# Two 64x64 steps in one slot, and a w_out product that lags two FFN steps

## The chip, the cores and the metric

The kernel runs on one core of a Trainium2 chip. The metric is the device time of one execution in microseconds (us); the time before is the median of three runs. A core has a matrix engine (TensorE, in the profile PE, with its weight loads as PEld), three engines for everything else (VectorE or DVE, ScalarE or ACT, GpSimd or POOL), and SyncE (SP), which here only issues transfers. Each engine works through its own list of instructions in order and waits on semaphores for the others. TensorE writes to PSUM; VectorE and ScalarE read the results from there.

## The reference

A long convolution of each channel, made from a small filter network, is followed by a feed-forward block (FFN) with three input products and a maximum. Four sequences of 12544 positions, 128 channels, all in fp32:

```python
h_filt = (np.maximum(pos_emb @ w1, 0.0) @ w2) * window      # one filter per channel
u = x * v
y = irfft(rfft(u, n=2*S, axis=1) * rfft(h_filt, n=2*S, axis=0), n=2*S, axis=1)[:, :S, :]
a = (x * y).reshape(B * S, D)                               # 50176 x 128
h = np.maximum(np.maximum(a @ moe_w1, a @ moe_w2), a @ moe_w3)   # 50176 x 768
out = h @ moe_w_out                                         # 50176 x 128
```

The kernel computes the transforms as matrix products, in several steps of which one, in the frequency domain, is done in blocks of 64x64. The maximum of three is turned into a maximum of two: one input product is subtracted from the weights of the other two ahead of time, and its own share of the output is one further product with a matrix `lin`.

## The kernel before

The program has a prologue (filter, transforms of sequence 0), a middle stage, and a last stage (the FFN of sequence 3). In the middle stage the FFN of sequence b runs while the convolution of sequence b + 1 is computed beside it. The FFN goes through 32 tiles of 392 columns for each sequence, with 6 steps of 128 hidden units each. So there are 192 steps ("slots") for each sequence, and the work of the convolution is dealt out to these slots.

One FFN step is `up` and, one step later, `down`:

```python
    def up(i, f, tag="hid", bufs=3):
        ...
        pa = hps.tile([P, 512], FP32, tag="hps", name="pa")        # hps: 3 PSUM buffers
        halves_mm(pa[:, 0:N], w_sb[1][:, f * P:(f + 1) * P], rhs, True, True)
        nc.scalar.activation(h[:], pa[:, 0:N], Relu)
        pb = hps.tile([P, 512], FP32, tag="hps", name="pb")
        halves_mm(pb[:, 0:N], w_sb[2][:, f * P:(f + 1) * P], rhs, True, True)
        nc.vector.tensor_tensor(out=h[:], in0=h[:], in1=pb[:, 0:N], op=ALU.max)
        return h

    def down(i, f, h):
        if f == 0:
            pos_[i] = ops.tile([D, 512], FP32, tag="ops", name="ops")   # one PSUM buffer
            halves_mm(pos_[i][:, 0:N], lin[:], ...)
        halves_mm(pos_[i][:, 0:N], wo_sb[:, f, :], h[:], False, f == NF - 1)
        if f < NF - 1:
            return
        ...
        nc.scalar.copy(o[:].rearrange("d p n -> d (p n)"), pos_.pop(i)[:, 0:N])
        nc.gpsimd.dma_start(dst, o[:])
```

`halves_mm` makes each product as two of 128x64. A step of the convolution in the frequency domain (for g, forward; for z = g - 3, backward) is made of products of 64x64. Its result is folded out of PSUM; then come the swaps, two multiplications with the filter, a sum on GpSimd, and the unfolding:

```python
    def g_quarter(g, z):                                    # TensorE, 2 x 16 matmuls
        ps = cps.tile([P, 1024], FP32, tag="cv", name="psq")   # cps: 2 PSUM buffers
        ...  nc.tensor.matmul(ps[64 * a:64 * a + 64, at:at + D], w[64 * r:64 * r + 64, k, a, :],
                              t[64 * r:64 * r + 64, k, a, :], ...)      # psq<-sq,wt
        ...  nc.tensor.matmul(ps[64 * k:64 * k + 64, at:at + D], w[64 * a:64 * a + 64, k, q, :],
                              ab[64 * a:64 * a + 64, q, k, :], ...)     # psq<-xs,wt

    def g_fold(g, z):                                       # ScalarE, VectorE twice
        nc.scalar.copy(eo[:, lo:hi], ps[:, 512 + lo:512 + hi])
        for a, op in enumerate((ALU.add, ALU.subtract)):
            nc.vector.tensor_tensor(out=cb[:, a, lo:hi], in0=ps[:, lo:hi], in1=eo[:, lo:hi], op=op)

    def q_swap(g, at): ...     # ScalarE, two of 32 rows
    def q_re(g): ...           # VectorE: cb * ht
    def q_im(g): ...           # VectorE: xs * ht, then GpSimd: cb + xs
    def q_unfold(g, q): ...    # VectorE, half of it each
```

`conv_steps` deals these out to slots (here the part for the frequency domain; `at(slot, late, function, ...)`, where late = 1 puts an entry at the end of its slot):

```python
        for x in range(NK + LATE):                          # 45 + 3 steps
            s = s0 + int(x * per_pair)                      # per_pair: about 2.5 slots
            g, z = x if x < NK else None, x - LATE if x >= LATE else None
            at(s, 1, g_quarter, g, z)
            at(s + 1, 0, g_fold, g, z)
            at(s - 4, 0, w_load, x)
            ...
```

Each tile of the FFN also needs its own transform back. `t_load` fetches zt; `t_sums` makes a sum and a difference on GpSimd, or on VectorE (two `scalar_tensor_tensor`) in the second half of sequences 1 to 3; `t_last` makes 32 small matmuls into yps, in a buffer of the same `cps`, and multiplies the result with x into gt:

```python
        for f in range(NF):
            if i < NT - 2:
                if f == 0:
                    t_load(*tiles[n + 2])
            ...
            turn_ = i == NT - 1
            if f == (3 if turn_ else 1):
                t_sums(tiles[n + 1], nc.vector if turn_ else nc.gpsimd)
            ...
            h = up((b, i), f)
            if late is not None:
                down(*late)
            late = ((b, i), f, h)
            if f == (4 if turn_ else 3):
                t_last(tiles[n + 1])
            ...
            run(beside.pop(s, ()))                          # the slot's convolution work
```

Of the kernel before, what the change touches and what calls it, by code (L numbers as in the profile page):

```python
# [27 lines left out]
LATE = 3  # L28
# [61 lines left out]
def kernel(  # L90
# [20 lines left out]
    NF = DFF // P  # L111
    NK = N1 // 2
# [37 lines left out]
    def halves_mm(out, lhsT, rhs, start, stop):  # L150


        for h in range(2):
            nc.tensor.matmul(out[64 * h:64 * h + 64], lhsT[:, 64 * h:64 * h + 64], rhs,  # L154
                             start=start, stop=stop, skip_group_check=True)
# [416 lines left out]
    def conv_steps(b, done):  # L572


        out = []

        def at(slot, late, fn, *args):
            out.append((slot, late, len(out), fn, args))

        per_pair = 170 / (NK + LATE + 0.6 * (NU - done))
        for u in range(done, NU):
            s = (u - done) * 0.6 * per_pair + 9
            at(max(0, int(s) - 9), 0, u_load, b, u)
            at(int(s) - 6, 0, u_mul, u)
            at(int(s) - 5, 0, u_planes, u)
            at(int(s) - 4, 0, u_dma, u)
            at(int(s), 0, u_join, u)
            at(int(s + 1), 1, u_first, u)  # L590
        s0 = int((NU - done - 1) * 0.6 * per_pair + 9) + 6
        load = [(1.2 if i % NF == 3 else 0.6) + (1.4 if i % NF == 1 and b > 1 and i >= NT * NF // 2 else 0)
                for i in range(NT * NF)]
        for x in range(NK + LATE):
            load[s0 + int(x * per_pair) + 1] += 1.4

        def emptiest(among, cost):
            s = min(among, key=lambda i: load[i])
            load[s] += cost
            return s  # L600

        for x in range(NK + LATE):
            s = s0 + int(x * per_pair)
            g, z = x if x < NK else None, x - LATE if x >= LATE else None
            at(s, 1, g_quarter, g, z)
            at(s + 1, 0, g_fold, g, z)
            at(s - 4, 0, w_load, x)
            if z is not None:
                at(s + 3, 0, g_store, b, z)
            if g is None:  # L610
                continue
            if g % 2 == 0:
                at(s - 4, 0, q_load, g, min(2, NK - g))
                at(s - 1, 0, h_load, g, min(2, NK - g))
            at(s + 2, 0, q_swap, g, 0)
            at(s + 3, 0, q_swap, g, 64)
            last = s0 + int((x + LATE) * per_pair) - 1
            a = emptiest(range(s + 4, min(s + 5, last - 2) + 1), 0.7)
            at(a, 0, q_re, g)
            a = emptiest(range(a, min(s + 6, last - 1) + 1), 0.7)  # L620
            at(a, 0, q_im, g)
            for q in range(2):
                at(emptiest(range(a + 1, last + 1), 0.55), 0, q_unfold, g, q)
        slots = {}
        for s, _, _, fn, args in sorted(out, key=lambda r: r[:3]):
            slots.setdefault(s, []).append((fn, args))
        return slots


    N = 4 * NB  # L630
    NT = P // 4
# [26 lines left out]
    def t_sums(i, eng=nc.gpsimd):  # L658
        z0, z1 = zts[i]
        even = hp.tile([N1, 512], FP32, tag="even", name="even", bufs=2)  # L660
        if i[0] == 0 or i[1] < NT // 2:
            eng.tensor_tensor(out=even[:], in0=z0, in1=z1, op=ALU.add)
            eng.tensor_tensor(out=z1, in0=z0, in1=z1, op=ALU.subtract)
        else:
            for out, op in ((even[:], ALU.add), (z1, ALU.subtract)):
                nc.vector.scalar_tensor_tensor(out=out, in0=z1, scalar=sign_t[:, 0:1], in1=z0,
                                               op0=ALU.mult, op1=op)
        zts[i] = even[:], z1
# [31 lines left out]
    def down(i, f, h):  # L700
        if f == 0:
            pos_[i] = ops.tile([D, 512], FP32, tag="ops", name="ops")
            halves_mm(pos_[i][:, 0:N], lin[:], gs[i][:].rearrange("d p n -> d (p n)"), True,
                      False)
# [3 lines that stand above are left out]
        gs.pop(i)  # L708
        o = op_.tile([D, 4, NB], FP32, tag="o", name="ot")
        nc.scalar.copy(o[:].rearrange("d p n -> d (p n)"), pos_.pop(i)[:, 0:N])  # L710
        dst = outT.rearrange("d (p b n) -> d p b n", b=B, n=NB)[:, 4 * i[1]:4 * i[1] + 4, i[0], :]
        nc.gpsimd.dma_start(dst, o[:])  # L712
# [94 lines left out]
    def run(steps):  # L807
        for fn, args in steps:
            fn(*args)
# [50 lines left out]
    for f in range(0, FO, 4):  # L860
        quad([hs[:, f + i] for i in range(4)], f1h[:], specH[:, :, :, f:f + 4])
        u, k = divmod(f // 4, 4)
# [10 lines left out]
    for u in range(0, NU, 2):  # L873
        t = uts.pop(u)
        for v in range(2):
            if u + 4 < NU:
                u_mul(u + 4 + v)
            at = 4 * (u + v)
# [77 lines left out]
    EARLY = 6  # L956
# [69 lines left out]

    tiles = [(b, i) for b in range(B) for i in range(NT)]
    LAST = (B - 1) * NT
    late = None
    for n, (b, i) in enumerate(tiles[:LAST]):  # L1030
        if i == 0:
            beside = {}
            beside = conv_steps(b + 1, EARLY if b == 0 else 0)
        if n == 0:
            t_load(*tiles[0])
            t_load(*tiles[1])
            t_sums(tiles[0], nc.vector)
            t_last(tiles[0])
# [5 lines that stand above are left out]
            elif i == NT - 1 and f < 2 and n + 1 + f < len(tiles):  # L1044
                t_load(*tiles[n + 1 + f])
            turn_ = i == NT - 1
            if f == (3 if turn_ else 1):
                t_sums(tiles[n + 1], nc.vector if turn_ else nc.gpsimd)
            if f == 4 and n + 1 == LAST:
                t_sums(tiles[n + 2], nc.vector)  # L1050
            h = up((b, i), f)
            if late is not None:
                down(*late)
            late = ((b, i), f, h)
            if f == (4 if turn_ else 3):
                t_last(tiles[n + 1])
            if f == 5 and n + 1 == LAST:
                t_last(tiles[n + 2])
            s = i * NF + f
            run(beside.pop(s, ()))  # L1060
            if s == NT * NF - 1:
                assert not beside, sorted(beside)
    first = up((B - 1, 0), 0)
    down(*late)
    conv.close()


# [20 lines left out]
    step, b = 0, B - 1  # L1088
    for i in range(0, NT, 2):
        h = {}  # L1090
# [63 lines left out]
```

## Time and profile before

| | before |
|---|---|
| median of 3 runs | 2351.22 us (2349.06 to 2354.83) |
| span of the profiled execution | 2351.5 us |
| prologue | to about 333 us |
| middle stage | about 333 to 1931 us |
| last stage | from about 1931 us |
| hid (L697, VectorE) | 768 times, 558 ns each |
| hid (L694, ScalarE) | 768 times, 499 ns each |
| psq matmuls | 4320 in 144 steps |
| eo (L484, ScalarE), cb (L487, VectorE) | 581 and 680 ns each (medians) |

In the profile a group reads "line engine operation out<-in", with the names of the program's buffers: pa and pb are the two input products, ops the product with w_out (or lin), psq the 64x64 products, ps the first transform, yps the transform back. In a timeline the first number is the start and the second the time from the first start to the last end of the instructions merged into that line, both in us. Matmuls are pipelined, so each is still draining when the next has begun, and the second number is longer than the distance to the next start. A bracket at the end gives how long the engine had been idle and what ended that. In a list of waits the three numbers are the total in us, how often, and the longest in us.

### The profile page before, as it was taken

What the parts mean: (1) busy time and instruction counts of PE and PEld (TensorE: products, weight loads), DVE (VectorE), ACT (ScalarE), POOL (GpSimd) and SP (SyncE); (2) the same over time, 40 slices, a digit from 0 to 9 for tenths busy, and PEclk for the clock granted to TensorE, in tenths of its full rate; (3) what the DMA queues carried; (4) which work ended last, traced back from release to release, by engine and by line L of the source; (5) the groups of instructions that cost most, each with busy time, mean ns of one, the idle gap of its engine ahead of it and who ended that gap; (6) DMA issues with size and microseconds to landing.
All of it is one profiled execution on the core that took longest, in us unless ns stands there. A gap on an engine that the chain in (4) does not pass through costs nothing.

```text
span 2351.5 us, 67998 instructions
## 1 busy us (share of the span) xinstructions
PE 2300.1 (98%) x27853; PEld 1373.9 (58%) x27853; DVE 1528.8 (65%) x2798; ACT 1172.7 (50%) x2124; POOL 976.0 (42%) x1153
## 2 busy tenths in 40 slices
PE   8999989999999999999999999999999999999998
PEld 7889866655545546654454446655454546666665
DVE  5668857756777747757787747757777755444443
ACT  2678844456665624446666624446666632222222
POOL 1045424334444434434333324434333326666666
PEclk9999999999999999999999999999999999999999
DMA  7869969979898869969899849969899922222221
GB/s 163 195 192 267 292 154 187 165 173 230 225 240 218 206 126 190 187 144 239 226 236 240 221 114 190 187 139 241 229 231 242 229 81 70 56 54 66 68 54 22
DMA packets 473145, 410.92 MB, mean 175 GB/s; under 512 B 328004, under 2 KB 374231, under 8 KB 472834
## 3 DMA queue, kind: packets, MB, share of 16 engines
q1 hardware_dynamic: 433504, 317.61, 60.9%
q0 software_dynamic: 26400, 75.72, 11.1%
q10 hardware_dynamic: 12930, 13.25, 1.8%
q8 instruction: 219, 3.59, 0.7%
q14 instruction: 92, 0.75, 0.1%
HBM read 262.77 MB, written 84.67 MB: 148 GB/s over the span
## 4 chain that ended last, share of the span: by engine, by line
PE 87%; DMA 5%; DVE 2%; issue 2%; ACT 2%; SPq 0%; POOL 0%; ACTq 0%; POOLq 0%; DVEq 0%
PE pa L154 20%; PE pb L154 19%; PE ops L154 16%; PE ops L757 6%; PE ps L408 5%; PE yps L154 5%; PE psq L462 3%; PE ps L163 3%; PE ps L154 3%; PE psq L472 2%; PE gps L926 1%; PE sps L944 1%; DMA zt<-zd 1%; DMA wt<-wq_const 1%; PE pm L323 1%
## 5 line engine op out<-in xcount | busy, mean ns | idle before, releaser
L694 ACT ACTIVATE hid<-pa 128x392 f32<-128x392 f32 x768 | 383.4, 499 | 683.0 <-PE pa L154 657.3
L697 DVE TENSOR_TENSOR hid<-hid,pb 128x392 f32<-128x392 f32 x768 | 428.7, 558 | 425.6 <-PE pb L154 332.5
L154 PE MATMUL pa<-gt,w_sb 128*64 128x392 f32 x3072 | 648.3, 499 | 0.8 <-DVE gt L684 0.8
L154 PE MATMUL pb<-gt,w_sb 128*64 128x392 f32 x3072 | 638.9, 493 | 3.6 <-ACT hid L694 3.6
L154 PE MATMUL ops<-hid,wo_sb 128*64 128x392 f32 x2304 | 478.9, 493 | 15.6 <-DVE hid L697 15.6
L154 PEld LDWEIGHTS pb<-gt,w_sb 128*64 128x64 f32 x3072 | 223.3, 137 | 288.2 <-issue 271.0
L514 POOL TENSOR_TENSOR cb<-cb,xs 128x512 f32<-128x512 f32 x135 | 174.9, 1296 | 444.5 <-DVE xs L511 155.0
L154 PEld LDWEIGHTS ops<-hid,wo_sb 128*64 128x64 f32 x2304 | 165.7, 137 | 232.6 <-issue 168.4
L154 PEld LDWEIGHTS pa<-gt,w_sb 128*64 128x64 f32 x3072 | 196.1, 137 | 137.8 <-issue 93.2
L712 POOL DMA_DIRECT2D out_dram<-ot x96 | 74.6, 777 | 422.4 <-ACT ot L710 285.8
L502 ACT ACTIVATE xs<-cb 32x512 f32<-32x512 f32 x270 | 169.5, 628 | 111.5 <-DVE cb L487 107.3
L487 DVE TENSOR_TENSOR cb<-psq,eo 128x512 f32<-128x512 f32 (+1 forms) x288 | 175.1, 649 | 72.5 <-ACT eo L484 72.5
L419 DVE TENSOR_TENSOR spec<-ps,high 128x360 f32<-128x360 f32 (+1 forms) x204 | 142.0, 738 | 114.3 <-ACT high L417 113.8
L503 ACT COPY xs<-cb 32x512 f32<-32x512 f32 x270 | 166.3, 616 | 3.1
L417 ACT COPY high<-ps 128x360 f32<-128x360 f32 (+1 forms) x102 | 77.3, 762 | 170.2 <-PE ps L408 112.7
L408 PEld LDWEIGHTS ps<-f1q,uT 98*64 98x64 f32 x3072 | 132.2, 137 | 34.6 <-issue 32.4
L154 PEld LDWEIGHTS yps<-f4p,even 90*64 90x64 f32 x2048 | 116.3, 138 | 41.0 <-issue 36.4
L408 PE MATMUL ps<-f1q,uT 98*64 98x90 f32 x3072 | 136.6, 241 | 3.1 <-DVE spec L419 2.6
L684 DVE TENSOR_TENSOR gt<-yps,xT 128x392 f32<-128x392 f32 x128 | 72.5, 567 | 97.7 <-PE yps L154 55.6
L154 PE MATMUL yps<-f4p,even 90*64 90x49 f32 x2048 | 125.6, 221 | 3.3 <-DMA f4p<-f4p_const 3.3
L154 PE MATMUL yps<-f4p,zt 90*64 90x49 f32 x2048 | 127.4, 223 | 0.0
L518 DVE TENSOR_TENSOR xs<-cb 128x256 f32<-128x256 f32 x270 | 115.9, 468 | 3.6 <-POOL cb L514 3.1
(130 smaller groups left out, 3343.0 us busy)
## 6 DMA issues: line engine op xcount, KB each, us to landing
ht<-hd SPq DMA_DIRECT2D x264, 256.0 KB, 5.9
wt<-wq_const SPq DMA_DIRECT2D x144, 256.0 KB, 6.7
zd<-cb POOLq DMA_DIRECT2D x135, 256.0 KB, 6.1
zt<-zd SPq DMA_DIRECT2D x384, 90.0 KB, 3.2
sq<-spec SPq DMA_DIRECT2D x264, 128.0 KB, 7.2
ut<-in_xr_dram SPq DMA_DIRECT2D x128, 196.0 KB, 4.1
ut<-in_vr_dram SPq DMA_DIRECT2D x128, 196.0 KB, 4.3
xT<-in_x_dram SPq DMA_DIRECT2D x256, 98.0 KB, 4.0
```

The lines of the kernel that those rows point to most:

```text
L154: nc.tensor.matmul(out[64 * h:64 * h + 64], lhsT[:, 64 * h:64 * h + 64], rhs, start=start, stop=stop, skip_group_check=True)
L408: nc.tensor.matmul(ps[64 * c:64 * c + 64, 256 * i + h * N1:256 * i + (h + 1) * N1], t[:, 2 * ((at + i) % 8) + h].rearrange("n r t -> n (r ...
L417: nc.scalar.copy(high, v[:, 0])
L419: nc.vector.tensor_tensor(out=spec[:, :, a, at:at + n], in0=v[:, 1], in1=high, op=op)
L487: nc.vector.tensor_tensor(out=cb[:, a, lo:hi], in0=ps[:, lo:hi], in1=eo[:, lo:hi], op=op)
L502: nc.scalar.mul(xs[at:at + 32], xt[at + 32:at + 64], -1.0)
L503: nc.scalar.copy(xs[at + 32:at + 64], xt[at:at + 32])
L514: nc.gpsimd.tensor_tensor(out=xts[g], in0=xts[g], in1=xs[:], op=ALU.add)
L518: nc.vector.tensor_tensor(out=ab[:, q], in0=y[:, 0], in1=y[:, 1], op=(ALU.subtract, ALU.add)[q])
L694: nc.scalar.activation(h[:], pa[:, 0:N], Relu)
L697: nc.vector.tensor_tensor(out=h[:], in0=h[:], in1=pb[:, 0:N], op=ALU.max)
L757: nc.tensor.matmul(ps[64 * c:64 * c + 64, 0:H2], w, rhs[:, H2 * c:H2 * c + H2], start=start, stop=True, skip_group_check=True)
```

## The change

Three things are changed, all for the middle stage. (1) Two steps of 64x64 products share a slot, one behind the other, where before each had its own; both start at `start(x)`, and the second step's fold, swaps and store follow one or two slots later than the first's. It is for going half as often from the FFN's products to the 64x64 products and back. (2) `down` runs two steps behind `up` in place of one, to give `hid` longer. (3) The transform of the next tile is placed around the pairs: its sums go to step 0, and `t_last` keeps out of the slot in which a pair's first fold stands. The diff:

```diff
--- before.py
+++ after.py
@@ -589,10 +589,16 @@
             at(int(s), 0, u_join, u)
             at(int(s + 1), 1, u_first, u)
         s0 = int((NU - done - 1) * 0.6 * per_pair + 9) + 6
-        load = [(1.2 if i % NF == 3 else 0.6) + (1.4 if i % NF == 1 and b > 1 and i >= NT * NF // 2 else 0)
+
+        def start(x):
+            return s0 + int(x // 2 * 2 * per_pair)
+
+        load = [(1.2 if i % NF == 3 else 0.6) + (1.4 if i % NF == 0 and b > 1 and i >= NT * NF // 2 else 0)
                 for i in range(NT * NF)]
         for x in range(NK + LATE):
-            load[s0 + int(x * per_pair) + 1] += 1.4
+            s = start(x)
+            load[s] -= 1.2
+            load[s + 1 + x % 2] += 1.4
 
         def emptiest(among, cost):
             s = min(among, key=lambda i: load[i])
@@ -600,31 +606,32 @@
             return s
 
         for x in range(NK + LATE):
-            s = s0 + int(x * per_pair)
+            s, odd = start(x), x % 2
             g, z = x if x < NK else None, x - LATE if x >= LATE else None
             at(s, 1, g_quarter, g, z)
-            at(s + 1, 0, g_fold, g, z)
+            at(s + 1 + odd, 0, g_fold, g, z)
             at(s - 4, 0, w_load, x)
             if z is not None:
-                at(s + 3, 0, g_store, b, z)
+                at(s + 3 + odd, 0, g_store, b, z)
             if g is None:
                 continue
             if g % 2 == 0:
                 at(s - 4, 0, q_load, g, min(2, NK - g))
                 at(s - 1, 0, h_load, g, min(2, NK - g))
-            at(s + 2, 0, q_swap, g, 0)
-            at(s + 3, 0, q_swap, g, 64)
-            last = s0 + int((x + LATE) * per_pair) - 1
-            a = emptiest(range(s + 4, min(s + 5, last - 2) + 1), 0.7)
+            first = s + 2 + 2 * odd
+            at(first, 0, q_swap, g, 0)
+            at(first + 1, 0, q_swap, g, 64)
+            last = start(x + LATE) - 1
+            a = emptiest(range(first + 1, min(first + 3, last - 1) + 1), 0.7)
             at(a, 0, q_re, g)
-            a = emptiest(range(a, min(s + 6, last - 1) + 1), 0.7)
+            a = emptiest(range(a, min(first + 4, last - 1) + 1), 0.7)
             at(a, 0, q_im, g)
             for q in range(2):
                 at(emptiest(range(a + 1, last + 1), 0.55), 0, q_unfold, g, q)
         slots = {}
         for s, _, _, fn, args in sorted(out, key=lambda r: r[:3]):
             slots.setdefault(s, []).append((fn, args))
-        return slots
+        return slots, {start(x) + 1 for x in range(NK + LATE)}
 
 
     N = 4 * NB
@@ -1026,11 +1033,10 @@
 
     tiles = [(b, i) for b in range(B) for i in range(NT)]
     LAST = (B - 1) * NT
-    late = None
+    late = []
     for n, (b, i) in enumerate(tiles[:LAST]):
         if i == 0:
-            beside = {}
-            beside = conv_steps(b + 1, EARLY if b == 0 else 0)
+            beside, folds = conv_steps(b + 1, EARLY if b == 0 else 0)
         if n == 0:
             t_load(*tiles[0])
             t_load(*tiles[1])
@@ -1044,15 +1050,17 @@
             elif i == NT - 1 and f < 2 and n + 1 + f < len(tiles):
                 t_load(*tiles[n + 1 + f])
             turn_ = i == NT - 1
-            if f == (3 if turn_ else 1):
+            if f == 0:
+                when = 4 if turn_ else min((3, 4, 2), key=lambda k: i * NF + k in folds)
+            if f == (3 if turn_ else 0):
                 t_sums(tiles[n + 1], nc.vector if turn_ else nc.gpsimd)
             if f == 4 and n + 1 == LAST:
                 t_sums(tiles[n + 2], nc.vector)
             h = up((b, i), f)
-            if late is not None:
-                down(*late)
-            late = ((b, i), f, h)
-            if f == (4 if turn_ else 3):
+            late.append(((b, i), f, h))
+            if len(late) > 2:
+                down(*late.pop(0))
+            if f == when:
                 t_last(tiles[n + 1])
             if f == 5 and n + 1 == LAST:
                 t_last(tiles[n + 2])
@@ -1061,7 +1069,8 @@
             if s == NT * NF - 1:
                 assert not beside, sorted(beside)
     first = up((B - 1, 0), 0)
-    down(*late)
+    for l in late:
+        down(*l)
     conv.close()
```

## The prediction

> **What bounds the kernel now.** I read the page first: busy times, slices, chain.
>
> ```profile
> PE 2300.1 (98%) x27853; PEld 1373.9 (58%) x27853; DVE 1528.8 (65%) x2798; ACT 1172.7 (50%) x2124; POOL 976.0 (42%) x1153
> PE   8999989999999999999999999999999999999998
> ...
> PEclk9999999999999999999999999999999999999999
> PE 87%; DMA 5%; DVE 2%; issue 2%; ACT 2%; SPq 0%; POOL 0%; ACTq 0%; POOLq 0%; DVEq 0%
> ```
>
> TensorE is busy in every slice, at full granted clock, and is 87% of the chain that ended last. So the time is the sum of what TensorE issues, plus the moments in which it waits. Matmuls overlap in their tails, so a busy time hides small losses. I therefore read the timeline of TensorE in the middle stage (about 333 to 1931 us), where the FFN of one sequence runs beside the convolution of the next, by the distance from start to start:
>
> ```profile
> 1089.76 0.83 PE L154 MATMUL pb<-gt,w_sb 128*64 128x392 f32 x4
> 1090.42 0.83 PE L154 MATMUL ops<-hid,wo_sb 128*64 128x392 f32 x4
> 1091.17 0.67 PE L462 MATMUL psq<-sq,wt 64*64 64x128 f32 x16
> 1091.66 0.62 PE L472 MATMUL psq<-xs,wt 64*64 64x128 f32 x16
> 1092.21 0.88 PE L154 MATMUL pa<-gt,w_sb 128*64 128x392 f32 x4
> 1092.92 0.83 PE L154 MATMUL pb<-gt,w_sb 128*64 128x392 f32 x4
> 1093.58 0.83 PE L154 MATMUL ops<-hid,wo_sb 128*64 128x392 f32 x4
> ```
>
> One FFN product takes 0.66 us from its start to the next (pb to ops, 1089.76 to 1090.42). But the ops before a psq takes 0.75 (1090.42 to 1091.17), and the pa after it 0.71 (1092.21 to 1092.92), with nobody to wait for in between. That is the cost of going into and out of the 64x64 products. Next the waits of TensorE:
>
> ```profile
> PE ops L154 <- DVE hid L697: 15.6, 13, 1.8
> PE pb L154 <- ACT hid L694: 3.6, 1, 3.6
> PE yps L154 <- DMA f4p<-f4p_const: 3.3, 1, 3.3
> ```
>
> 13 waits of the w_out product for hid are the only ones inside the middle stage that matter; the other two lines are its entry and its exit. One of the 13, first on TensorE, then on VectorE:
>
> ```profile
> 1115.83 0.83 PE L154 MATMUL pa<-gt,w_sb 128*64 128x392 f32 x4
> 1116.48 0.83 PE L154 MATMUL pb<-gt,w_sb 128*64 128x392 f32 x4
> 1119.07 0.88 PE L154 MATMUL ops<-hid,wo_sb 128*64 128x392 f32 x4 [1.76 <-DVE hid L697]
> ```
>
> ```profile
> 1115.82 1.29 DVE L487 TENSOR_TENSOR cb<-psq,eo 128x512 f32<-128x512 f32 x2 [2.43 <-ACT eo L484]
> 1117.02 0.74 DVE L666 SCALAR_TENSOR_TENSOR even<-zt,sign 90x512 f32<-90x512 f32 x1
> 1117.80 0.75 DVE L666 SCALAR_TENSOR_TENSOR zt<-zt,sign 90x512 f32<-90x512 f32 x1
> 1118.46 0.55 DVE L697 TENSOR_TENSOR hid<-hid,pb 128x392 f32<-128x392 f32 x1
> ```
>
> VectorE waited 2.43 us for ScalarE's copy eo, then did the fold (1.29) and the two sums of the next tile (1.5), and only then the hid that TensorE stood waiting for.
>
> **What the Trainium skill says.** "TensorEngine Tiling (Array Packing)", Key Properties: changing the tiling mode, not just the tile, drains TensorE. The trace agrees and gives the size: the FFN works in 128x64 tiles, psq in 64x64, and about 0.1 us is lost on each side. "TensorE: Matmul & The Clock Gate", Step-by-step: the queue pulls a weight load ahead of matmuls in flight when row groups do not conflict or the background buffer is free. Inside the FFN the trace shows this (loads of ops 0.33 us before its matmuls); the loads of psq start together with its first matmul, so on entry there is nothing pulled ahead. Same page, Architectural detail: the queues of ScalarE and VectorE are strict FIFO. The four VectorE lines above are just that: hid stands behind a fold whose input was late.
>
> **The change, part by part.**
>
> 1. Pairing. Before, 48 steps per sequence (45, and 3 late ones) for 3 sequences are 144 visits to the 64x64 mode; after, two steps share a visit: 72. What one visit loses, from the starts above at finer grain:
> - entry: 1090.42 to 1091.17 less 0.658 = 0.10;
> - inside, the steady rate: the second run of 16 spans 0.62 from first start to last end, the last matmul takes 0.269 (the median of psq), so the last start is 0.35 after the first; four start together within 0.02, which leaves 0.33 for three steps, 0.11 each, and 0.44 for 16. The first run takes 0.49: 0.05 over. The second takes 0.547 (median) to the start of pa: 0.11 over, the exit;
> - pa takes 0.709 in place of 0.658: 0.05.
>
> Sum 0.10 + 0.05 + 0.11 + 0.05 = 0.31 us, all on TensorE and so all on the path. 72 visits fewer give 72 x 0.31 = 22.5 us. No matmul is added or removed.
>
> 2. Lag. The product with w_out now comes two steps after its hid. That does not give a whole step of slack: pa and pb share three PSUM buffers, so pa of step n+2 reuses the buffer of pb of step n, which VectorE's hid must have read. The wait for hid moves from ops to that pa, one product later: 0.66 us of slack more, and more where a psq pair (about 2 us) or yps (0.9 us) stands between.
>
> 3. Placement. The sums of the next tile go from FFN step 1 to step 0, so they no longer sit between a fold and the hid of step 1; the copy of ops (which ScalarE holds its queue for) goes from step 0 to step 1 by the lag, so the two no longer meet. The transforms back (yps) avoid the slot after a pair, where both PSUM buffers are still full. Folds of a pair are in two following slots, and the first of them follows a slot of about 2.0 + 1.9 us, in which VectorE and ScalarE can catch up.
>
> The 13 waits are, from start to start, 8 of about 1.9 and 5 of about 0.5, some 17.8 us. Were only the 0.66 gained, 8 x 1.26 = 10 us would stay. With the sums elsewhere I expect most to go. What I expect anew: a pair in step 3 puts the second fold into step 5, just ahead of the sums of step 0. ScalarE: hid, two swaps 1.25, eo 0.59, so eo ends some 3.2 us into that slot; fold 1.3, sums 1.5, hid 0.56 end at 6.6, against the pa that needs it at about 5.9: 0.7 us, some four times (in the second half of two sequences). With other small meetings I put 5 us, a guess around 3 to 8. So the waits give 17.8 - 5 = 13 us.
>
> Sum: 2351.2 - 22.5 - 13 = 2316 us (-1.5%).
>
> **The rivals.**
>
> A. The pair waits inside. An even step's result, folded at slot s+1, is now needed by the second half of the next pair, 5 slots on (before: about 7.6). Its swaps, two products, GpSimd sum (1.3 us) and unfold (2 x 0.4) must fit in. And both halves need a PSUM buffer: with yps in a pair's slot, the second half waits until VectorE has multiplied it out (0.57). Against it: the unfold is placed in slot s+4 and the product comes at the end of s+5, about 2.4 us after the unfold's place, with 1 us of it to spare; and the first half of the pair takes 0.97 us, as long as the multiplication with its semaphores. For it: GpSimd is in order and holds its queue for stores. If each of 72 pairs waited 0.3 us, 22 us would be given back: about 2335.
>
> B. The waits only move: VectorE stays the engine behind, pa waits in place of ops, and 10 us or more remain: about 2321 to 2325.
>
> C. Transfers come late: weights of the second step of a pair reuse the buffer of the first step of the pair before, so their load is issued only then, with about 12 us to go; a load of wt lands in a median of 6.7 us. I hold that as hidden. Late loads of sq cost under 1 us before, and their lead is unchanged.
>
> D. More comes: no waits at all in the middle stage, and the small ones of psq (2 us) gone too: 2351 - 22.5 - 17.8 - 2 = 2309. The entry (3.3 us for f4p) and the exit (3.6 us, ScalarE waits for the last store before its buffer is reused) stay in any case.
>
> **Range and chances.** D is the floor, 2309; a little under for the spread of the runs (2349 to 2355). A and B together, in part, give 2328. So 2316, from 2308 to 2328. 2% faster would be 2304.2, under the floor of everything that I can count: 0.04. 2% slower needs 47 us of new waits, 0.65 us for each pair: 0.01. Within 2%: 0.95.
>
> **What would show it.** In the profile after: pairs of psq as x16, x16, x16, x16 between FFN products, with a visit of 0.49 + 0.44 + 0.44 + 0.55 = 1.92 us, entry and pa as before (0.10 and 0.05). If the pairs take 1.92 but the entry grows, the drain is not what I take it for. In TensorE's waits: ops no longer waits for hid; a line of pa waiting for hid of a few us is B, lines of psq waiting for xs, sq or a fold over 5 us in sum are A. The stages before 333 and after 1931 us should take the same time. I am wrong if those stages move by more than a few us, or if the sum of TensorE's waits in the middle stage does not fall.

## The result and the profile after

| | before | after |
|---|---|---|
| median of 4 runs each | 2351.38 us (2349.06 to 2354.83) | 2339.78 us (2339.31 to 2344.28) |
| ratio, 95% interval | | 0.9954 [0.9936, 0.9971] |
| span of the profiled execution | 2351.5 us | 2337.5 us |
| middle stage, first pa to the exit | 332.7 to 1931.4: 1598.7 us | 329.8 to 1917.3: 1587.4 us |
| last stage | 420.1 us | 420.2 us |

The change brings 11.6 us, where 35 were predicted and 23 was the least that the range allowed. The last stage has not moved. The prologue ends 3 us earlier here, but it ends anywhere between 327 and 333 us in the runs below, which leave it unchanged too. So what follows is about the middle stage: 11.3 us shorter, where 35.3 (22.5 + 12.8) were expected. From here on its length is given beside each median, because it is free of the prologue's spread. It comes from one trace for each kernel, though: the last stage, which no edit touches, took 418.6 to 421.0 us in the 14 traces, so a difference of 2 or 3 us between two traces shows little.

First the page of the kernel after (busy times, chain; its rows of PE and of the clock are the same as before, digit for digit):

```profile
PE 2284.1 (98%) x27853; PEld 1371.9 (59%) x27853; DVE 1553.8 (66%) x2798; ACT 1178.8 (50%) x2124; POOL 969.0 (41%) x1153
...
PE 76%; DMA 11%; DVE 5%; issue 3%; ACT 2%; SPq 1%; POOL 0%; ACTq 0%; DVEq 0%; POOLq 0%
```

The bound is the same. Two numbers should make the reader look further: VectorE (DVE) is busy 25 us longer with the same 2798 instructions, and its share of the chain went from 2% to 5%. (The share of transfers, DMA, rose as well, but in the middle stage TensorE itself waits only 0.4 us for one, twice for weights.) TensorE in the timeline after, around one pair of steps:

```profile
631.53 0.83 PE L154 MATMUL ops<-hid,wo_sb 128*64 128x392 f32 x4
632.29 0.67 PE L462 MATMUL psq<-sq,wt 64*64 64x128 f32 x16
632.78 0.62 PE L472 MATMUL psq<-xs,wt 64*64 64x128 f32 x16
633.22 0.62 PE L462 MATMUL psq<-sq,wt 64*64 64x128 f32 x16
633.94 0.45 PE L472 MATMUL psq<-xs,wt 64*64 64x128 f32 x8
635.35 0.45 PE L472 MATMUL psq<-xs,wt 64*64 64x128 f32 x8 [0.96 <-DVE xs L518]
635.73 0.88 PE L154 MATMUL pa<-gt,w_sb 128*64 128x392 f32 x4
636.44 0.83 PE L154 MATMUL pb<-gt,w_sb 128*64 128x392 f32 x4
```

The pair is there, with the predicted 0.49 (632.29 to 632.78) and 0.44 (to 633.22), the entry of 0.76 and the pa of 0.71. But the fourth run of 16 is torn in two: its second half stands waiting for `xs`, the unfolded result of an earlier step. From the last start before the gap (634.12) to 635.35 it is 1.23 us, of which the trace counts 0.96 as waiting: three times what the pair saves. The waits of TensorE after:

```profile
PE pb L154 <- ACT hid L701: 10.2, 12, 3.5
PE psq L472 <- DVE xs L518: 9.6, 15, 1.0
...
PE psq L472 <- DVE gt L691: 3.0, 1, 3.0
```

The line "ops waits for VectorE's hid", 15.6 us before, is gone. Three others came: pb waits for ScalarE's hid (10.2 us, of which the 3.5 are the exit as before), psq for xs, and psq, once, for gt. The prediction's rival A named the waits of psq, for xs and (0.57 us) for gt; nothing named the wait of pb. The idle time of TensorE in the middle stage, without entry and exit, was 18.2 us before and is 21.3 us after: by the prediction's own sign ("if the sum of TensorE's waits in the middle stage does not fall") it is wrong.

**The wait of pb.** The timeline at its second occurrence, TensorE and then ScalarE:

```profile
343.74 0.84 PE L154 MATMUL pa<-gt,w_sb 128*64 128x392 f32 x4
345.16 0.88 PE L154 MATMUL pb<-gt,w_sb 128*64 128x392 f32 x4 [0.59 <-ACT hid L701]
```

```profile
344.61 0.50 ACT L701 ACTIVATE hid<-pa 128x392 f32<-128x392 f32 x1 [1.48 <-PE pa L154]
```

That hid reads pa, of the same step, from PSUM, and pb starts when it has read it (344.61 + 0.50 is 345.11). pb depends on nothing in that hid, except if both have the same PSUM buffer. The addresses in the built program say so: in 10 of the 768 steps pa and pb share one of the three buffers (in the kernel before: in none). The pool does not deal them out strictly in turn, and with two steps of lag the order that it arrives at is another. Such a step runs 1.42 us from pa to pb (343.74 to 345.16) in place of 0.66; two of the ten run 1.73 us. All ten together: 8.3 us from start to start.

**The wait for xs.** VectorE around 630 us, with GpSimd below it:

```profile
630.64 4.66 DVE L518 TENSOR_TENSOR xs<-cb 128x256 f32<-128x256 f32 x3
```

```profile
630.39 1.27 POOL L514 TENSOR_TENSOR cb<-cb,xs 128x512 f32<-128x512 f32 x1 [5.32 <-ACT hid L701]
...
632.23 1.37 POOL L669 TENSOR_TENSOR even<-zt 90x512 f32<-90x512 f32 x1
633.67 1.34 POOL L670 TENSOR_TENSOR zt<-zt 90x512 f32<-90x512 f32 x1
```

Three unfolds, 0.42 us each by the median, take 4.66 us, and beside each stands a sum on GpSimd. The Trainium skill has this, on the page "SBUF — State Buffer", section "Who interferes with whom": a VectorE instruction with two SBUF inputs contends with a GpSimd instruction that reads SBUF, and whoever issues first blocks the other; a GpSimd instruction that only writes does not contend. The trace agrees that one blocks the other: the second of the three unfolds runs from 631.87 to 633.89 and ends 0.29 us after GpSimd's even (632.23 + 1.37), and every one of the 65 stretched unfolds of this trace ends 0.28 to 0.29 us after the end of a GpSimd sum, as if it could only then do most of its 0.42 us. Who issues first is less clear: in 58 of the 65 the sum had started first, but in 7, this one among them, the unfold has the earlier start, by up to 0.37 us. The group of the unfolds, of the kernel before and then of the kernel after (behind the bar: busy us in all, mean ns):

```profile
L518 DVE TENSOR_TENSOR xs<-cb 128x256 f32<-128x256 f32 x270 | 115.9, 468 | 3.6 <-POOL cb L514 3.1
```

```profile
L518 DVE TENSOR_TENSOR xs<-cb 128x256 f32<-128x256 f32 x270 | 167.5, 662 | 9.8 <-POOL cb L514 9.8
```

The same 270 instructions: 14 of them over 0.62 us before, 65 after. 43 of the 65 have GpSimd's sum of the two products (cb<-cb,xs) beside them, which with pairs falls into slots where another step is being unfolded; 22 have the sums of the next tile (even, zt). The unfolds were counted in the prediction as "2 x 0.4".

The one wait of psq for gt comes from the same place. VectorE makes gt out of yps and so frees its buffer; here gt and a hid stand behind three stretched unfolds:

```profile
818.19 4.64 DVE L518 TENSOR_TENSOR xs<-cb 128x256 f32<-128x256 f32 x3
822.76 0.55 DVE L704 TENSOR_TENSOR hid<-hid,pb 128x392 f32<-128x392 f32 x1
823.23 0.55 DVE L691 TENSOR_TENSOR gt<-yps,xT 128x392 f32<-128x392 f32 x1
```

The two causes explain most of it: 8.3 us from the shared buffers, and about 17 us that the psq products take longer from start to start than where they hardly wait (151.9 in the kernel after, 134.8 in the best version below). What the waits cost is a reading so far. The experiments test it.

### The profile page after: what moved, and what is told of

Its sections match the earlier page's. It is cut to its first block, busy times and chain, and to the rows that moved or that the text cites. A ratio compares the mean times of both kernels' runs of the same rounds, so it can differ in the third digit from the quotient of the medians.

```text
span 2337.5 us, 68165 instructions
## 1 busy us (share of the span) xinstructions
PE 2284.1 (98%) x27853; PEld 1371.9 (59%) x27853; DVE 1553.8 (66%) x2798; ACT 1178.8 (50%) x2124; POOL 969.0 (41%) x1153
## 4 chain that ended last, share of the span: by engine, by line
PE 76%; DMA 11%; DVE 5%; issue 3%; ACT 2%; SPq 1%; POOL 0%; ACTq 0%; DVEq 0%; POOLq 0%
PE pa L154 18%; PE pb L154 17%; PE ops L154 14%; PE ops L764 6%; PE ps L408 5%; DMA ht<-hd 4%; PE yps L154 4%; PE ps L163 3%; PE ps L154 2%; DMA zt<-zd 2%; PE psq L472 2%; DVE xs L518 2%; PE psq L462 2%; DMA sq<-spec 2%; DMA wt<-wq_const 1%
## 5 line engine op out<-in xcount | busy, mean ns | idle before, releaser
L154 PE MATMUL pb<-gt,w_sb 128*64 128x392 f32 x3072 | 640.3, 495 | 10.2 <-ACT hid L701 10.2
L518 DVE TENSOR_TENSOR xs<-cb 128x256 f32<-128x256 f32 x270 | 167.5, 662 | 9.8 <-POOL cb L514 9.8
```

Of the source, the lines that this page charges most:

```text
L518: nc.vector.tensor_tensor(out=ab[:, q], in0=y[:, 0], in1=y[:, 1], op=(ALU.subtract, ALU.add)[q])
```

## The experiments

| run | median us | ratio to before | middle stage us |
|---|---|---|---|
| before | | 1 | 1598.7 |
| lag only | 2341.55 | 0.9965 [0.9954, 0.9975] | 1591.8 |
| lag only, fixed rotation | 2339.72 | 0.995 [0.9935, 0.9965] | 1586.6 |
| the same, memset for the sum* | 2332.70 | 0.9916 [0.9902, 0.9931] | 1581.0 |
| pairs and placement, lag of one | 2346.54 | 0.9986 [0.998, 0.9993] | 1594.2 |
| after | 2339.78 | 0.9954 [0.9936, 0.9971] | 1587.4 |
| after, tile sums in step 1 | 2334.69 | 0.9917 [0.9902, 0.9932] | 1582.5 |
| after, fixed rotation | 2332.88 | 0.9932 [0.9917, 0.9947] | 1579.9 |
| ... odd unfolds early | 2330.49 | 0.9917 [0.9899, 0.9934] | 1577.0 |
| ... odd unfolds and tile sums placed | 2325.04 | 0.9893 [0.9876, 0.991] | 1571.7 |
| ... transform back later as well | 2321.73 | 0.9865 [0.9849, 0.9881] | 1566.4 |
| ... VectorE's tile sums placed as well | 2329.46 | 0.9892 [0.9875, 0.9908] | 1578.2 |
| after, memset for the sum* | 2323.80 | 0.9892 [0.9876, 0.9909] | 1569.0 |
| ... and fixed rotation* | 2318.04 | 0.9865 [0.9846, 0.9884] | 1563.0 |

The three with * leave out the imaginary part of the filter, so their times are no times of the kernel; they say what the sum costs. Each kernel ran 4 to 20 times, each time with the kernel before beside it for the ratio. Differences of medians from separate sets of runs are less certain than the ratios, so the argument goes by ratios and by the middle stage of the traces.

### The lag alone

The kernel before, with `down` two steps behind `up`, and nothing else:

```diff
-    late = None
+    late = []
...
-            if late is not None:
-                down(*late)
-            late = ((b, i), f, h)
+            late.append(((b, i), f, h))
+            if len(late) > 2:
+                down(*late.pop(0))
...
-    down(*late)
+    for l in late:
+        down(*l)
```

> Only the lag of two steps, on the kernel before; no pairs, the sums of the next tile stay in step 1. Theory 1 (the lag is worth its slack, and harms by the way PSUM buffers are dealt out): the 13 waits of ops for hid (17.8 us from start to start) shrink to 0 to 10 us, and six steps in which pa and pb now hold the same PSUM buffer add 0.76 us each, 4.6 us: 2338 to 2348 us. Rival (the waits only move from ops to pa): pa waits for hid about as long as ops did, and the time is 2350 us or more.

Measured: the waits of ops for hid are gone, and the middle stage is 6.9 us shorter, not 17.8. The list of waits has a new line:

```profile
PE pb L154 <- ACT hid L694: 7.2, 7, 3.6
```

Without the 3.6 of the exit: 6 waits, and in 6 steps pa and pb share a buffer. So the sharing comes with the lag and needs no pairs. pa does not wait for hid, against the rival. And of the 270 unfolds 29 are stretched in place of 14, all beside the sums of even and zt: a lag alone moves the engines against one another.

### Pairs and placement with a lag of one

```diff
             late.append(((b, i), f, h))
-            if len(late) > 2:
+            if len(late) > 1:
                 down(*late.pop(0))
```

> The changed kernel with the product with w_out one step behind again; pairs and placement stay. Theory 1 (pairs gain 22.5 us and lose about half of that again in waits for the unfolded xs; the lag brings a few us): psq waits for xs about 10 us as in the changed kernel, no step has pa and pb in one buffer, ops waits for hid again for some 5 to 18 us: 2338 to 2348 us. Rival (the lag is worth nothing here and only brought the shared buffers): 2330 to 2334 us, with ops waiting for hid under 3 us.

The first line of TensorE's waits in it:

```profile
PE ops L154 <- DVE hid L704: 16.1, 34, 1.1
```

No buffer is shared, but ops waits for hid 34 times, as long in sum as in the kernel before in 13: the placement alone does not keep VectorE in time. The lag is worth 6.8 us here (1594.2 to 1587.4) and was worth 6.9 alone. Pairs and placement without it bring 4.5 us. The expectation was wrong in one point: psq waits for xs 5.0 us in 6, not about 10, although 65 unfolds are stretched here too. So the number of stretched unfolds alone does not say how long TensorE waits.

### Three PSUM buffers in fixed rotation

The kernel after with pa and pb dealt from three named buffers in turn:

```diff
+    turns_ = [0]
+
+    def hps_tile(name):
+        turns_[0] += 1
+        return hps.tile([P, 512], FP32, tag=f"hps{turns_[0] % 3}", name=name, bufs=1)
...
-        pa = hps.tile([P, 512], FP32, tag="hps", name="pa")
+        pa = hps_tile("pa")
...
-        pb = hps.tile([P, 512], FP32, tag="hps", name="pb")
+        pb = hps_tile("pb")
```

> The changed kernel with the three PSUM buffers of pa and pb in a fixed rotation, so that pa and pb of one step never hold the same one. Theory 1: the 10 waits of pb for ScalarE's hid in the middle stage (6.7 us of waiting, 7.9 from start to start) are gone, and the time is 2330 to 2334 us. Rival (the wait is only put off to the next product or to the unfold): within 2 us of the changed kernel, 2338 to 2342 us.

```profile
PE pb L154 <- ACT hid L707: 3.3, 2, 3.2
PE pa L154 <- DVE hid L710: 3.3, 6, 0.6
```

The waits of pb are gone but for the exit (3.2) and a trace, and the middle stage is 7.6 us shorter, nearly what the ten shared steps cost (8.3). In their place pa waits for hid, six times by 0.55 us: this is the wait that the prediction put at "0.7 us, some four times", and it could show only once the rotation was the one assumed there. The wait of psq for xs stays (6.5 us in 8).

### The lag alone, in fixed rotation

> The kernel before with the lag of two steps and the fixed rotation, no pairs. Theory 1: the 6 steps with pa and pb in one buffer gone, 4 to 5 us less than the lag alone: 2335 to 2338 us. Rival: the same as the lag alone, 2341 us.

The same edit on the kernel with the lag only: 1591.8 to 1586.6, 5.3 us for 6 shared steps. Together with the run before: 0.8 to 0.9 us for each shared step, with pairs and without. By the medians it is less sure: 2339.72 us lies above the expected range, 1.8 us under the lag alone, and the two ratios overlap.

### A memset in place of GpSimd's sum

The kernel after, with a write-only instruction where GpSimd adds the two products (the imaginary part is left out):

```diff
-        nc.gpsimd.tensor_tensor(out=xts[g], in0=xts[g], in1=xs[:], op=ALU.add)
+        nc.gpsimd.memset(xts[g], 0.0)
```

> The changed kernel with GpSimd's sum cb + xs replaced by a memset of cb to zero: GpSimd still writes cb and the unfold still waits for it, but GpSimd reads nothing from SBUF; the product's imaginary part is left out. Theory 1 (GpSimd's reads hold up VectorE's instructions with two inputs in SBUF): the 43 unfolds that took about 1.3 us beside that sum take 0.42, psq waits for xs fall from 9.6 to under 4 us, and the time is 2330 to 2335 us. Rival (the unfold is late because the chain of swaps, multiplications and sum is too long for 5 slots): the waits for xs stay over 7 us and the time within 3 us of the changed kernel.

```profile
L518 DVE TENSOR_TENSOR xs<-cb 128x256 f32<-128x256 f32 x270 | 125.5, 508 | 0.0
```

Not one unfold is stretched beside the memset; the 22 beside the tile sums are left. psq no longer waits for xs, and the middle stage is 18.4 us shorter (16.0 by the medians), more than expected. The run has a weakness: the memset is also shorter (0.52 against 1.3 us) and doesn't wait for VectorE's second product, so the unfolds could come in time for that reason alone, and a memset turns out to gain 5.5 us without pairs as well (below). So the 18.4 us are not all the collision's. The next runs keep the sum.

### Odd steps unfolded early

On the kernel in fixed rotation, the unfolds of a pair's second step are held to the two slots after its sum is placed, where they had any slot up to the step that needs them:

```diff
+            until = min(a + 2, last) if odd else last
             for q in range(2):
-                at(emptiest(range(a + 1, last + 1), 0.55), 0, q_unfold, g, q)
+                at(emptiest(range(a + 1, until + 1), 0.55), 0, q_unfold, g, q)
```

> Pairs, lag and fixed rotation; the unfolds of the second step of a pair one or two slots after its multiplications, ahead of GpSimd's sum for the next pair's first step, in place of beside it. All work is done. Theory 1 (a VectorE instruction with two inputs in SBUF is held up by GpSimd's reads): of the 43 unfolds stretched by that sum fewer than 15 are left, psq waits for xs fall from 6.5 us to under 3, and the time from 2333 to 2325 to 2330 us. Rival (the load on VectorE is what counts, and it is the same): waits of another kind come up and the time stays within 2 us of 2333.

No unfold has GpSimd's sum beside it any more, but 33 have the tile sums, 11 more than before the edit; pa waits for hid 5.8 us in place of 3.3. psq still waits for xs 3.7 us, more than expected. The middle stage is 2.9 us shorter only, which the spread could make, and the ratios overlap. Taking the collision away in one place made it in another. So both kinds of sum have to be placed.

### Both sums placed

As the last, with both odd unfolds two slots behind their sum, and GpSimd's sums of the next tile in that one of the steps 0 to 2 which comes soonest after a pair, while VectorE still folds:

```diff
+                u = min(a + 2, last) if odd else emptiest(range(a + 1, last + 1), 0.55)
+                at(u, 0, q_unfold, g, q)
...
+            if f == 0:
+                def after_pair(k):
+                    past = [s for s in starts if s <= i * NF + k]
+                    d = i * NF + k - past[-1] if past else 1
+                    return (1, 2, 3, 4, 0).index(d) if d < 5 else 0
+                pool = b == 0 or i + 1 < NT // 2
+                sums = 3 if turn_ else min((0, 1, 2), key=after_pair) if pool else 0
-            if f == (3 if turn_ else 0):
+            if f == sums:
```

> As e5, with the second step's unfolds always two slots after its multiplications, and GpSimd's sums of the next tile (where GpSimd makes them) in step 0, 1 or 2, whichever follows a pair soonest, so that they run while VectorE folds out of PSUM. Theory 1: the 22 unfolds stretched by the sums of the next tile fall to under 10 as well, the 3 us wait of psq for gt goes, and the time is 2319 to 2326 us. Rival (the sums only hold up the two multiplications in place of the unfolds): no better than e5.

6 unfolds are stretched, psq doesn't wait for xs at all, and the wait for gt is gone (0.2 us). With all the work done, it is 8.2 us shorter than in fixed rotation alone (1579.9 to 1571.7), and 2325.04 us beat both kernels. Compared with the run before, the unfolds of a pair's second step come later here (they end 5.2 us after VectorE's second product by the mean, in place of 3.7); what moved away is the tile sums. So the waits are not gone because the unfolds come sooner. What it bought:

```profile
PE yps L154 <- POOL zt L671: 3.5, 5, 1.1
```

The transform back (yps) comes before the later sums have ended, in five places.

### The transform back after the sums

```diff
-                when = 4 if turn_ else min((3, 4, 2), key=lambda k: i * NF + k in folds)
+                when = 4 if turn_ else min((3, 4), key=lambda k: (i * NF + k in folds, pool and k < sums + 2))
```

> The kernel with GpSimd's sums after the pair, and in addition the transform back at least two steps after those sums. Theory: the 3.5 us in 5 waits of yps for GpSimd's zt were bought by the later sums and go; the rest stays. So 2319 to 2323 us, and no line of yps waiting for zt over 1 us. Rival: yps then comes later and holds its PSUM buffer into the next pair, and the waits only change their name: within 2 us of 2325.

```profile
PE yps L154 <- POOL zt L671: 2.2, 2, 1.1
```

Three of the five waits are gone, two of 1.1 us are left: the keeping out of a fold's slot ranks first in that key. The middle stage is 5.3 us shorter (the medians differ by 3.3, and the ratios just overlap), more than the 1.3 us that this line lost; the DMA waits of psq, 1.9 us before, fell to 0.2. The collision has no part in it: 11 unfolds are stretched, 5 more than in the run before. This is the best version: 2321.73 us, 0.9865 of the time before [0.9849, 0.9881]. It does all that the kernel before does. The mean of its unfolds is back where it was before the change:

```profile
L518 DVE TENSOR_TENSOR xs<-cb 128x256 f32<-128x256 f32 x270 | 111.6, 454 | 51.9 <-POOL cb L514 51.7
```

VectorE now sits idle 51.7 us before unfolds, waiting for GpSimd's sum, and no more of it reaches TensorE: psq does not wait for unfolds, and pa waits for hid 3.3 us as in fixed rotation alone.

### VectorE's tile sums placed as well

In the second half of a sequence VectorE makes the tile sums, always in step 0. Here they are placed too, preferring the slot right after a pair, then the pair's own:

```diff
-                    return (1, 2, 3, 4, 0).index(d) if d < 5 else 0
+                    return ((1, 2, 3, 4, 0) if pool else (1, 0, 4, 2, 3)).index(d) if d < 5 else 0
...
-                sums = 3 if turn_ else min((0, 1, 2), key=after_pair) if pool else 0
+                sums = 3 if turn_ else min((0, 1, 2), key=after_pair)
```

> As the one before, and the tile sums that VectorE makes (second half of a sequence) are also placed by the distance from the pair. Theory: the six waits of pa for hid (3.3 us) come from the sums in step 0 right behind a second fold and go: 2316 to 2321 us. Rival: VectorE's sums meet swaps, unfolds or the product with x in the other step, and nothing is gained: within 2 us of the one before.

```profile
PE psq L462 <- DMA wt<-wq_const: 4.8, 7, 1.8
...
PE yps L154 <- DVE zt L674: 3.3, 4, 0.8
```

Against the theory and its rival, it is 11.9 us longer in the middle stage (7.7 by the medians). pa's waits for hid fell from 3.3 to 0.7 us, as the theory had it, but yps now waits for the sums (3.3 us) and for the buffer of a fold (2.9 us in 5), and the weights of psq come late (4.8 us). For VectorE's sums, step 0 was the better place here.

### The tile sums back in step 1

The kernel after with one part of its placement undone:

```diff
-            if f == (3 if turn_ else 0):
+            if f == (3 if turn_ else 1):
```

> The changed kernel with the sums of the next tile put back to step 1: the placement undone for the sums alone. Theory: the sums meet folds of pairs in step 1 and 2 again, and with two steps of lag this shows as waits of pa or ops for hid, 3 to 10 us more: 2342 to 2350 us. Rival: with the lag there is slack enough and the placement of the sums is worth nothing: 2338 to 2341 us.

Against both the theory and its rival, it is faster than the kernel after: 0.9917 [0.9902, 0.9932] against 0.9954 [0.9936, 0.9971], and 4.9 us in the middle stage. pa and ops do not wait for hid, and the wait of psq for xs is shorter than the 9.6 us of the kernel after:

```profile
PE psq L472 <- DVE xs L518: 5.2, 10, 1.0
```

Stretched unfolds are 51 in place of 65. So the move of the sums to step 0, which was to shorten waits, did not: with two steps of lag, hid is in time with the sums in either step. Why it cost time is only partly named. The waits for xs are 4.4 us shorter and the single wait of 3.05 us for gt is gone, but psq waits for gt 3.6 us in four other places and for weights 2.5 us more, so that all waits of TensorE in the middle stage are only 1.0 us shorter (20.3 in place of 21.3). Another 1.7 us is the clock, which is at half after the long wait for gt (last section). About 2 us stay open.

### What a pair is worth by itself

The kernel after in fixed rotation and with the memset, and the kernel with the lag only and the same two edits, differ by the pairs and the placement:

> The changed kernel with the fixed rotation and with GpSimd's sum replaced by a memset (the imaginary part is left out). Theory 1 (the two costs that the prediction did not count are separate and add up): 2324 less 7 to 8, 2314 to 2319 us, about the time predicted for the changed kernel. Rival (they overlap): 2320 us or more.

> The kernel before with the lag and fixed rotation, steps single, and GpSimd's sum of the two products replaced by a memset: the imaginary part of the filter is left out. It is the partner of the run with pairs, rotation and memset (2318.04 us, middle stage 1563.0), and differs from that by the pairs and the placement alone. Theory: a pair saves 0.31 us, 22.5 us in sum, and single steps never had GpSimd's sum beside an unfold, so the memset gives nothing here: middle stage about 1585.5, 2337 to 2341 us. Rival: the memset frees GpSimd and VectorE also with single steps, so that part of the difference to the run without memset was not the pairs': middle stage under 1580, below 2334 us.

Middle stages of 1563.0 and 1581.0 us: 18.0 us for the pairs and their placement, with waits of 4.9 us (pa for hid 2.9, psq for gt 2.0) in the first and 2.7 (psq) in the second; without these it would be about 20. The first median, 2318.04, is as expected from two costs that add up. The memset gave 5.5 us with single steps too (1586.6 to 1581.0): their unfolds beside tile sums fell from 29 to 11. So the second expectation was wrong in that, and the 23.6 us between the two runs without and with pairs (1586.6 and 1563.0) were not all the pairs'.

The visits themselves say it directly. From the start of the product ahead of psq to the start of the one behind the next pa, a visit of one step takes 2.502 us (median of 101, kernel before), one of two steps 3.376 (median of 50, kernel after). A pair in place of two single visits, with the two FFN products that now stand elsewhere, saves 2 x 2.502 - 3.376 - 2 x 0.658 = 0.31 us, and 72 of them 22.5 us. The mean of those 50 visits is 3.642: so 0.27 us of waits for each, nearly what it saves. In the best version the mean is 3.450.

## Why the prediction was wrong

**Pairing: right.** "72 x 0.31 = 22.5 us" (22.3 as written; 22.5 with 0.312): the visit after is 3.376 us by the median, and saves 0.31. Nothing grew at the entry or in pa. The two whole kernels above give about 20 us for it, so the sum is confirmed less closely than the single visit.

**Lag: right in what it removes, wrong in an assumption.** All 15.6 us of waits of ops for hid went, in every run with a lag of two, and in no other. But "pa and pb share three PSUM buffers, so pa of step n+2 reuses the buffer of pb of step n" holds for a strict rotation, and the pool does not rotate strictly. Ten steps with both products in one buffer cost 7.6 to 8.3 us. The order of buffers was fixed in the program and needed no run to be read; it was assumed.

**Placement and its waits: the step that failed.** "With the sums elsewhere I expect most to go ... With other small meetings I put 5 us, a guess around 3 to 8." Without any waits the middle stage would be 1598.7 - 22.5 - 17.8 = 1558.4 us; with the 5 us of new waits that this step allowed, 1563.4. Measured are 1587.4, so there are 29 us in place of 5: 8 from the buffers, some 17 in the psq visits, the rest not named. The waits guessed in detail (pa for hid, 0.7 us four times) were nearly right, 0.55 us six times, once the rotation was fixed. The sum failed in "other small meetings". The chain behind psq was weighed, in rival A, with durations taken singly (unfold 2 x 0.4, sum 1.3), while 65 unfolds take up to 2.0 us because GpSimd reads SBUF beside them. In the kernel before 14 were stretched too, so the trace had the sign: a mean of 468 ns beside a median of 417. Step by step, the fixed rotation gave back 7.6 us of the 24 that were missing, the placing of sums and unfolds 8.2, the later transform back 5.3.

That this is the cause of the waits for xs, and not a chain too long for its five slots, is shown from three sides: all 65 stretched unfolds end right behind a GpSimd sum; a write-only instruction in the sum's place ends the waits (with a gain of 18.4 us that is not all theirs); and so does moving the sums and unfolds apart with all the work left in (8.2 us).

**Rival A was half right.** It said "If each of 72 pairs waited 0.3 us, 22 us would be given back: about 2335". The size is right (0.27 us for each), and so is the place, psq waiting for xs. The argument against it, that the chain fits its slots, was right for undisturbed durations. It named GpSimd, but for being in order, not for blocking VectorE. The single wait for gt, which A put at 0.57 us, was 3.05, behind three stretched unfolds. It got too little of the range: 2335 lies outside it.

**B, C, D.** Waits of pa for hid (B) appear only in fixed rotation, 3.3 us (5.8 with the early unfolds). Late transfers (C): psq waits 0.4 us for wt in the kernel after; hidden, as held. The 47 us named for 2% slower leave out the 35 that the change was to gain: it would take some 82. The floor (D, 2309) was not reached by any version. With both causes out, the middle stage comes near the predicted 1563.4 us: 1563.0 with memset and rotation, and 1566.4 in the best full version. That the first agrees to 0.4 us is luck: the memset also gains what no prediction counted (5.5 us with single steps), and the pairs brought less than 22.5.

What stays open: where the 5.3 us of the last gain come from, beyond the 3 us of waits that can be named; what the memset gains beyond the waits for xs; and why the sums in step 1 meet fewer unfolds than in step 0, since no run moved GpSimd's tile sums without VectorE's.

## What to carry to other kernels

When a change moves work on VectorE and GpSimd against each other, don't add up undisturbed durations: look for two-input VectorE instructions whose mean is above their median, and at what GpSimd does beside them, and keep GpSimd's reading instructions out of those slots. An order that a pool decides (which PSUM buffer comes next) is read from the built program or forced by names, not assumed. And when one measure removes the reason for another (the lag for the move of the sums), try the change without the other.

## What the runs showed of the hardware beyond that

A long wait of TensorE can cost more than itself. The wait of psq for gt in the kernel after, and what follows:

```profile
823.84 0.67 PE L472 MATMUL psq<-xs,wt 64*64 64x128 f32 x16 [3.05 <-DVE gt L691]
...
825.35 1.53 PE L154 MATMUL pb<-gt,w_sb 128*64 128x392 f32 x4
826.65 1.53 PE L154 MATMUL ops<-hid,wo_sb 128*64 128x392 f32 x4
```

The products from 825.35 on stand 1.30 us apart, twice the 0.66. The stretch from 823 to 829 us of that trace, by engine (the third number from the end is the granted clock, 1.00 in the stretches of 6 us on both sides):

```profile
823.00:829.00 6.00, 5.16 (x34) 2.27 (x36) 2.01 (x5) 0.76 (x2) 0.49 (x1) 0.72 0.01 3
```

At 0.72 over 6 us the loss is 0.28 x 6 = 1.7 us on top of the wait. With the memset the same wait is 1.95 us, and the next products keep their 0.66:

```profile
815.70 0.67 PE L472 MATMUL psq<-xs,wt 64*64 64x128 f32 x16 [1.95 <-DVE gt L691]
816.29 0.88 PE L154 MATMUL pa<-gt,w_sb 128*64 128x392 f32 x4
817.00 0.83 PE L154 MATMUL pb<-gt,w_sb 128*64 128x392 f32 x4
```

The Trainium skill, "TensorE: Matmul & The Clock Gate", section "What's actually happening", gives about 3.4 us of idling for the drop to half. Here waits of 3.0 to 3.1 us were enough, in all three kernels with this wait, and the eight waits of 1.76 us in the middle stage before did nothing. But the length of one wait decides it neither way. In the run with VectorE's sums placed, a wait of 1.75 us was followed by the same drop:

```profile
1209.84 0.67 PE L462 MATMUL psq<-sq,wt 64*64 64x128 f32 x16 [1.75 <-DMA wt<-wq_const]
...
1211.94 1.53 PE L154 MATMUL pb<-gt,w_sb 128*64 128x392 f32 x4
```

In the run with the lag only, two waits of 1.04 and 0.33 us within one step of psq had the same effect once, while its wait of 3.58 us at the exit had none:

```profile
1919.81 0.88 PE L154 MATMUL pb<-gt,w_sb 128*64 128x392 f32 x4 [3.58 <-ACT hid L694]
1920.52 0.83 PE L154 MATMUL pa<-gt,w_sb 128*64 128x392 f32 x4
1921.18 0.83 PE L154 MATMUL pb<-gt,w_sb 128*64 128x392 f32 x4
```

Its last stage is also the shortest of all 14 (418.6 us, the others 420.1 to 421.0). What decides it besides the length, no run here shows.
